# Two transformer layers on one core: statistics a block ahead, a two-phase start, and a LayerNorm apply with a negated mean

## The chip, the cores and the metric

The kernel runs on one core of one Trainium2 chip. The metric is the device time of one execution in microseconds (us). "Median" is the median of the runs of a kernel, the profiled one among them. A profile is one execution; the same program profiled twice differed by 3 us, so differences of 2 or 3 us between the ends of single traces are not read.

Names: PE is TensorE, ACT is ScalarE, DVE is VectorE, POOL is GpSimd, SP is the engine that issues DMAs.

## The reference, cut to what matters

```python
def _layernorm(x, axis=-1, eps=1e-5):
    m = jnp.mean(x, axis=axis, keepdims=True)
    v = jnp.var(x, axis=axis, keepdims=True)
    return (x - m) / jnp.sqrt(v + eps)

# A: attention, 2048 tokens, width 512, 32 heads of 16.  B: gated feed-forward, 512 -> 1792 -> 512
x = A_x
x = x + _A_ref(_layernorm(x), A_wqkv, A_wo)
x = x + _B_ref(_layernorm(x), B_w_gate, B_w_up, B_w_down)
x = x + _A_ref(_layernorm(x), A_wqkv, A_wo)          # the same weights again
x = x + _B_ref(_layernorm(x), B_w_gate, B_w_up, B_w_down)
```

The heads are tiny (16), so the exponentials of the softmax weigh as much as the matmuls (in the profile of before, ACT is busy for 1605 us and PE for 1643): 2 layers x 32 heads x 2048 x 2048 of them.

## The kernel before

The kernel is written as a list scheduler. While the program is built, a model with a cost for each instruction decides in which order each engine gets its work; that order is then fixed. PE takes its instructions strictly in that order. So a cost in the model that is too low makes PE stand in front of an instruction whose input is not there, with everything behind it waiting.

The tokens are four blocks of 512. The width is four columns of 128 (`NCK`); a column serves two "units" of a block of queries. A unit is one block of 512 queries against all keys for four heads: 64 score tiles of 128x512, numbered by key tile and head, in groups of 12 tiles (three key tiles). There are 32 units in a layer, 64 in all. A score slot takes three tiles: either ACT does the exponential of all three, or ACT does two and DVE the third (an integer approximation) when it has time. Before units 2c and 2c+1 of layer 0 can run, column c must have its projections: a key, a value and, per block of queries, a query projection. For the first block of queries that makes 4 + 4 + 1 = 9 groups of matmuls per column.

The LayerNorm and its apply (`us` is the model's cost in us; 1.05 for POOL):

```python
def stats(i, rows, key, then=None, prio=1):
    dve(prio, [(lambda e: e.bn_stats(ST[:, i, :], rows), [key], [("ST", i)], 0.72),
               (lambda e: e.bn_aggr(MV[:, i, :], ST[:, i, :]), [("ST", i)], [("MV", i)], 0.1)], then)

def ln_scale(n, then, lo=0):                  # on POOL: 1/sqrt(var + eps) into row 1
    ...
    (lambda e: e.tensor_scalar(LNS[:, 0, lo:lo + n], var, LN_EPS, None, op0=ALU.add), ...
    (lambda e: e.tensor_tensor(LNS[:, 1, lo:lo + n], LNS[:, 0, lo:lo + n], CM05[:, 0:n], op=ALU.pow), ...

def ln_apply(i, rows, key, eng, alt, then=None, us=None):
    us = us or (1.05 if eng == "pool" else 0.46)
    job(eng, 1, [(lambda e: e.tensor_scalar(xn(i, alt), rows, MV[:, i, 0:1], LNS[:, 1, i:i + 1],
                                            op0=ALU.subtract, op1=ALU.mult), ...
```

The head, which brings in the four blocks, and the projections:

```python
def head_source(b):                           # one block: statistics, scale, apply, transposes
    ...
    if b > 1:
        while ("xnt", 0, b - 2) not in have:
            yield None
    for i, tt in enumerate(tts):
        stats(i, xb(tt), ("XB", tt), got(("st", name, i)), prio=0 if b == 0 else 1)
    for lo, n in parts:
        ...                                   # wait, ln_scale, wait, ln_apply on DVE
    for i, tt in enumerate(tts):
        ...
        yield transpose_piece(...)
    have.add(("xnt", 0, b))                   # block b is in

def kv(c, b):                                 # a column's key and value projection of block b
    def gate():
        return ("xnt", layer, b) in have and (...)
```

And the choice of what PE does next. Score matmuls come first, then matmuls of weights with values if there are many, then a "piece" of something else, if it fits before the next score matmuls are due. The last number is how much a piece may delay them:

```python
if bs is None or piece_ready(p, bs) > t + 0.02 or p.cost + change("full") > limit + src.tol():
    continue
...
sources = [Source(heads(), lambda: 0.1), Source(prep_source(), lambda: 0.1), Source(post_source(), post_tol)]
```

When PE has nothing, the program gives it dummy matmuls, meant to keep its clock up (`keep_clock`, tiles `fONB,fZV`).

## Time and profile before

| | before |
|---|---|
| median of the first three runs | 1774.62 us (1772.35 to 1775.3) |
| ACT busy | 1605 us, 90% |
| PE busy, dummies included | 1643 us, 93% |
| DVE busy | 1273 us, 72% |
| first exponential, end of the last one | 21.8 us, 1701.7 us |

The list of the costliest groups on the page, cut to two. The columns are: line of the program, engine, operation, output<-input, shape, count | busy us, mean ns | idle us of the engine just before them, and what ended it.

```profile
L1139 ACT ACTIVATE fPT<-fPS 128x1024 bf16<-128x1024 f32 (+1 forms) x1440 | 1531.5, 1200 | 95.6 <-PE fPS L1134 93.5
...
L555 POOL TENSOR_SCALAR fHT<-fX,fMV,fLNS 128x512 bf16<-128x512 f32 x36 | 75.3, 2106 | 0.9
```

The exponentials are nearly all of ACT's work, and nearly all of ACT's idle time in front of them (93.5 of 95.6 us) ended with a score matmul of PE. So the question is why PE was late. The timeline of ACT at the start (start, length, group, and in brackets the idle time before it):

```profile
21.82 13.54 ACT L1139 ACTIVATE fPT<-fPS 128x1536 bf16<-128x1536 f32 x10 [9.39 <-PE fPS L1134]
40.92 8.16 ACT L1139 ACTIVATE fPT<-fPS 128x1536 bf16<-128x1536 f32 x6 [5.57 <-PE fPS L1134]
50.10 32.91 ACT L1139 ACTIVATE fPT<-fPS 128x1536 bf16<-128x1536 f32 x32 [1.01 <-PE fPS L1134]
```

Ten three-tile exponentials take 13.54 us, 1.35 us each from one to the next. There are holes of 5.57 and 1.01 us while blocks 2 and 3 come in. It is worth seeing what PE did in the longer one, from 35.4 to 40.9 us (line 585 with `fWK`: key projections, four matmuls each; line 649: value projections, sixteen each):

```profile
34.25 1.90 PE L585 MATMUL fPS<-fXNT,fWK 128*128 128x512 bf16 x8
...
35.98 1.06 PE L649 MATMUL fPS<-fWV,fXNT 128*128 128x128 bf16 x16
...
37.30 1.07 PE L649 MATMUL fPS<-fWV,fXNT 128*128 128x128 bf16 x16
...
38.62 1.04 PE L585 MATMUL fPS<-fXNT,fWK 128*128 128x512 bf16 x4
39.50 1.06 PE L649 MATMUL fPS<-fWV,fXNT 128*128 128x128 bf16 x16
```

The second place is the LayerNorms that POOL applies, nine of them. Here is the first; first POOL, then ACT, then PE's longest waits over the whole run (total us, times, longest):

```profile
263.54 8.27 POOL L555 TENSOR_SCALAR fHT<-fX,fMV,fLNS 128x512 bf16<-128x512 f32 x4
```

```profile
271.07 1.45 ACT L1139 ACTIVATE fPT<-fPS 128x1536 bf16<-128x1536 f32 x1 [2.22 <-PE fPS L1134]
273.13 1.45 ACT L1139 ACTIVATE fPT<-fPS 128x1536 bf16<-128x1536 f32 x1 [0.61 <-PE fPS L1134]
276.04 1.45 ACT L1139 ACTIVATE fPT<-fPS 128x1536 bf16<-128x1536 f32 x1 [1.45 <-PE fPS L1134]
```

```profile
PE fPS L1134 <- ACT fPT L1139: 54.0, 198, 1.1
PE fPS L562 <- POOL fHT L555: 22.1, 27, 1.6
```

Four applies take 8.27 us, about 2.07 each, where the model allows 4.2. PE stands in front of the transposes (line 562) for 22.1 us in all, the score matmuls behind them come late, and ACT stands too. The windows query of the first three of these LayerNorms (length; busy us of PE, weight load, DVE, ACT, POOL; granted clock, DMA share, GB/s) shows a lower clock there too. That it comes with the waiting is shown by E1 below, where the waiting is gone and the clock at these three LayerNorms is 1.00:

```profile
263.00:279.00 16.00, 12.63 (x104) 3.95 (x96) 4.41 (x9) 11.49 (x9) 8.70 (x5) 0.79 0.02 4
415.00:431.00 16.00, 12.81 (x93) 3.49 (x89) 5.24 (x10) 10.88 (x11) 9.13 (x5) 0.68 0.25 67
480.00:498.00 18.00, 14.35 (x113) 4.35 (x106) 3.78 (x7) 13.19 (x11) 8.27 (x4) 0.81 0.05 15
```

ACT was busy 11.49 of 16 us in the first. Added up from the trace over the 16 us after the start of each of the nine applies, ACT was idle for 31.7 us.

### The profile page before, as it was taken

To read this page: it belongs to the slowest core of one execution; us is meant where nothing else is said; L and a number is where in the kernel's file an instruction comes from. 1 tells how busy PE (TensorE), PEld (TensorE's weight loads), DVE (VectorE), ACT (ScalarE), POOL (GpSimd) and SP (SyncE) were. 2 spreads that over 40 slices of the span, in tenths; PEclk is the share of its full clock that TensorE was granted. 3 is DMA by queue.
4 is the path that set the end of the run, shared out by engine and by line. 5 is a ranking of instruction groups with operands and counts; after the bars stand their busy time and mean duration, and the time that the engine had idled before them with its cause. 6 is when DMAs were issued, how large, how long until landed. Compare 5 with 4: busy or idle time off the path is not lost.

```text
span 1774.4 us, 38110 instructions
## 1 busy us (share of the span) xinstructions
PE 1643.3 (93%) x16129; PEld 495.7 (28%) x16129; DVE 1272.6 (72%) x2117; ACT 1605.2 (90%) x1486; POOL 243.1 (14%) x200
## 2 busy tenths in 40 slices
PE   9999998998899999999999999999988999899998
PEld 4232222222222223222332222222222222222233
DVE  7799985776756976549543999668786687855853
ACT  4999998998999999999899999899988999999932
POOL 2212021102201032010610111201012000201000
PEclk9999999998999999999999999999999999999999
DMA  4100001152012420143124000014301233013503
GB/s 131 49 2 17 2 18 42 53 164 59 16 43 82 150 53 13 46 126 108 47 66 143 2 18 18 25 49 121 111 18 31 58 108 111 21 43 88 149 19 103
DMA packets 140289, 111.89 MB, mean 63 GB/s; under 512 B 13904, under 2 KB 129872, under 8 KB 140112
## 3 DMA queue, kind: packets, MB, share of 16 engines
q1 hardware_dynamic: 136416, 104.78, 20.4%
q0 software_dynamic: 2112, 4.19, 0.9%
q8 instruction: 131, 2.15, 0.5%
q10 hardware_dynamic: 1584, 0.39, 0.1%
q14 instruction: 46, 0.38, 0.1%
HBM read 97.78 MB, written 6.82 MB: 59 GB/s over the span
## 4 chain that ended last, share of the span: by engine, by line
ACT 54%; PE 28%; DVE 11%; POOL 4%; issue 1%; DMA 1%; SPq 0%; POOLq 0%; DVEq 0%
ACT fPT L1139 50%; PE fPS L585 8%; PE fPS L1134 7%; PE fPS L1244 5%; DVE fPI L1173 5%; DVE fPP L1195 3%; POOL fHT L555 3%; PE fPS L943 3%; PE fPS L1264 3%; ACT fHT L1105 2%; DVE fQ L629 1%; PE fPS L649 1%; PE fPS L562 1%; POOL fLNS L545 1%; ACT L1105 1%
## 5 line engine op out<-in xcount | busy, mean ns | idle before, releaser
L1139 ACT ACTIVATE fPT<-fPS 128x1024 bf16<-128x1024 f32 (+1 forms) x1440 | 1531.5, 1200 | 95.6 <-PE fPS L1134 93.5
L1134 PE MATMUL fPS<-fQ,fKT 32*128 32x512 bf16 x4096 | 557.3, 388 | 69.3 <-ACT fPT L1139 54.0
L1173 DVE TENSOR_SCALAR fPI<-fPS 128x512 int16<-128x512 f32 x772 | 506.9, 683 | 89.4 <-PE fPS L1134 87.6
L1244 PE MATMUL fPS<-fPT,fVP 128*17 128x512 bf16 x3324 | 437.8, 388 | 3.8 <-DVE fPP L1195 2.0
L1195 DVE TENSOR_SCALAR fPP<-fPI 128x2048 int16<-128x2048 int16 x579 | 391.7, 711 | 6.6 <-PE fPS L1244 5.5
L1134 PEld LDWEIGHTS fPS<-fQ,fKT 32*128 32x128 bf16 x4096 | 139.6, 91 | 612.8 <-ACT fPT L1139 508.3
L1244 PE MATMUL fPS<-fPP,fVD 128*17 128x512 f16 x2316 | 297.7, 383 | 8.3 <-DVE fPP L1195 7.5
L1264 PE MATMUL fPS<-fONB,fZV 128*17 128x512 bf16 x3124 | 243.6, 389 | 2.4 <-POOL fQMASK L361 1.5
L585 PE MATMUL fPS<-fXNT,fWR 128*128 128x512 bf16 x896 | 232.2, 388 | 11.9 <-DVE fHT L929 9.0
L1244 PE MATMUL fPS<-fPI,fVP 128*17 128x512 f16 x772 | 214.3, 384 | 0.9 <-DVE fPP L1195 0.8
L929 DVE TENSOR_TENSOR fHT<-fPS,fHT 128x512 bf16<-128x512 f32 x112 | 76.9, 689 | 112.5 <-PE fPS L585 78.9
L778 POOL TENSOR_TENSOR fAT<-fOS,fRB 128x512 bf16<-128x512 f32 x32 | 40.9, 1278 | 814.5 <-DMA fRB<-rscr 814.5
L1244 PEld LDWEIGHTS fPS<-fPT,fVP 128*17 128x17 f16 x3324 | 98.9, 87 | 166.7 <-issue 125.3
L906 DVE CAST fHT<-fPS 128x512 bf16<-128x512 f32 x98 | 67.6, 690 | 96.2 <-PE fPS L585 96.2
L943 PE MATMUL fPS<-fWR,fHT 128*128 128x512 bf16 x448 | 123.6, 383 | 0.4
L585 PEld LDWEIGHTS fPS<-fXNT,fWR 128*128 128x128 bf16 x896 | 72.7, 98 | 130.0 <-DVE fHT L929 27.4
L1244 PEld LDWEIGHTS fPS<-fPP,fVD 128*17 128x17 f16 x2316 | 70.2, 88 | 94.1 <-issue 44.4
L1264 PEld LDWEIGHTS fPS<-fONB,fZV 128*17 128x17 f16 x3124 | 72.2, 91 | 75.8 <-issue 33.0
L555 POOL TENSOR_SCALAR fHT<-fX,fMV,fLNS 128x512 bf16<-128x512 f32 x36 | 75.3, 2106 | 0.9
L662 POOL TENSOR_SCALAR fVD<-fVP 128x544 f16<-128x544 f16 (+1 forms) x48 | 53.4, 1115 | 137.8 <-DVE fVP L670 135.1
L576 DVE COPY fXNT<-fPS 128x512 bf16<-128x512 bf16 x62 | 25.2, 422 | 61.9 <-PE fPS L562 61.7
L543 POOL TENSOR_SCALAR fLNS<-fMV 128x4 f32<-128x4 f32 (+1 forms) x17 | 7.6, 444 | 451.3 <-DVE fMV L537 451.3
(59 smaller groups left out, 732.6 us busy)
## 6 DMA issues: line engine op xcount, KB each, us to landing
fWR<-in_B_w_down_dram SPq DMA_DIRECT2D x189, 256.0 KB, 3.0
fWR<-in_B_w_gate_dram SPq DMA_DIRECT2D x56, 256.0 KB, 3.3
fWR<-in_B_w_up_dram SPq DMA_DIRECT2D x56, 256.0 KB, 2.8
fRB<-rscr SPq DMA_DIRECT2D x256, 32.0 KB, 1.9
fX<-in_A_x_dram POOLq DMA_DIRECT2D x4, 1024.0 KB, 5.7
xscr<-fX SPq DMA_DIRECT2D x16, 256.0 KB, 2.5
fX<-xscr SPq DMA_DIRECT2D x4, 1024.0 KB, 5.5
fAT<-fATS SPq DMA_DIRECT2D x128, 16.0 KB, 1.8
```

What stands on the lines that cost most here:

```text
L555: job(eng, 1, [(lambda e: e.tensor_scalar(xn(i, alt), rows, MV[:, i, 0:1], LNS[:, 1, i:i + 1], op0=ALU.subtract, op1=ALU.mult), [key, ("MV ...
L585: ins = e.matmul(bank(bs[0])[:, 0:cols], lhsT=l, rhs=r_, start=(i == 0), stop=(i == n - 1))
L662: job("pool", 2, [(lambda e, dst=dst, src=src, ph=ph: e.tensor_scalar(dst, src, 2.0 ** (-ph / NPH), None, op0=ALU.mult), [("VP", c, k) for ...
L906: evac_job(1, b, [(lambda e: e.tensor_copy(HT[:, ft, :], bank(b)), [BK[b]], [("HT", ft)], 0.6)], got(("gate", layer, qb, ft)))
L929: (lambda e: e.tensor_tensor(HT[:, ft, :], bank(b), HT[:, ft, :], op=ALU.mult), [BK[b], ("HT", ft)], [("HT", ft)], 0.62)], got(("up", laye ...
L943: ins = e.matmul(bank(b)[:, 0:D], lhsT=HT[:, ft, i * 128:(i + 1) * 128], rhs=WR[:, s, jj * D:(jj + 1) * D], start=(ft == 0), stop=(ft == N ...
L1134: ins = e.matmul(bank(b0 + k), lhsT=KT[32 * j:32 * j + 32, c, kt * 128:(kt + 1) * 128], rhs=Q[32 * j:32 * j + 32, qs, :], start=True, stop ...
L1139: o = sch.op("act", lambda e: e.activation(PT[:, p, 0:512 * na].rearrange("p (a b) -> p a b", a=na), PS[:, b0:b0 + na, :], ACTF.Exp, scale ...
L1173: dve(0, [(lambda e: e.tensor_scalar(PI[:, gi, 512 * r:512 * (r + 1)], bank(b0 + n - 1), DBIAS, 0.0, op0=ALU.add, op1=ALU.max), [bks[-1]], ...
L1195: shifts.append((s, [(lambda e: e.tensor_scalar(PP[:, s, :], PI[:, gi, :], int(OCT) * ph // NPH, None, op0=ALU.add), [("PI", gi, r) for r ...
L1244: ins = e.matmul(PS[32 * j:32 * j + VW, ACC, :], lhsT=l, rhs=r_, start=a, stop=z, tile_position=(0, 32 * j), skip_group_check=True)
L1264: ins = e.matmul(PS[32 * j:32 * j + VW, ACC, :], lhsT=ZV[:, :], rhs=ones, start=False, stop=False, tile_position=(0, 32 * j), skip_group_c ...
```

## The change

Its intent: bring the blocks in sooner and start the exponentials sooner. Statistics of a block are taken while the block before is worked on. The first two units do their first 12 tiles each before either goes on, so 24 tiles wait only for block 0. The score banks are kept for the scores once the first query projection is there. The second column's projections wait until all four blocks are in. DVE helps with exponentials only once all four blocks are in, where before it could from the second unit on. And the LayerNorm apply becomes add,multiply with a row that holds minus the mean, which costs one small POOL instruction per LayerNorm.

```diff
-    ST = sb("fST", [128, 4, 6], F32)           (MV and LNS likewise: 4 -> 8)
+    ST = sb("fST", [128, 8, 6], F32)
...
         pool_ -= held3
+        if slot_no[0] < 2 and (0, "q", 0) in have:
+            pool_.difference_update(slot_banks())
...
     def ln_scale(n, then, lo=0):
+        mean = AP(MV, 2 * lo, [[16, 128], [2, n]])
...
+            (lambda e: e.tensor_scalar(LNS[:, 2, lo:lo + n], mean, -1.0, None, op0=ALU.mult),
+             keys + [("LNS", lo + i) for i in range(n)], [("LNS", lo + i) for i in range(n)], 0.3)], then)
...
-        job(eng, 1, [(lambda e: e.tensor_scalar(xn(i, alt), rows, MV[:, i, 0:1], LNS[:, 1, i:i + 1],
-                                                op0=ALU.subtract, op1=ALU.mult),
-                      [key, ("MV", i), ("LNS", i)], [xnkey(i, alt)], us)], then, ported=True)
+        job(eng, 1, [(lambda e: e.tensor_scalar(xn(i, alt), rows, LNS[:, 2, st + i:st + i + 1], LNS[:, 1, st + i:st + i + 1],
+                                                op0=ALU.add, op1=ALU.mult),
+                      [key, ("LNS", st + i)], [xnkey(i, alt)], us)], then, ported=True)
...
+    def started_all():
+        return ("xnt", 0, NQB - 1) in have
...
-        def kv(c, b):
+        def kv(c, b, after_all=False):
             def gate():
-                return ("xnt", layer, b) in have and (
+                return ("xnt", layer, b) in have and (not after_all or started_all()) and (
...
-                return ("xnt", layer, up // NCK) in have and filled_units[0] >= layer * NU + 2 * up + 2 - NQS
+                return ("xnt", layer, up // NCK) in have and (layer or not up or started_all()) and filled_units[0] >= ...
...
-                    kv(up, b)
+                    kv(up, b, layer == 0)
...
-        if layer and NQB > 1:
-            for u in us[:NPART]:
-                unit(u, "A", 0, NMA, False)
...
+        if NQB > 1:
+            np_, m = (NPART, NMA) if layer else (2, 1)
+            for u in us[:np_]:
+                unit(u, "A", 0, m, False)
+            for u in us[:np_]:
+                unit(u, "B", m, NM, 4 * NKT > 12 * NM)
+            us = us[np_:]
...
-            d = size == 3 and (layer or u) and vector_group() and behind() < LAG
+            d = size == 3 and started_all() and vector_group() and behind() < LAG
...
+    def head_stats(b):
+        for i in range(4):
+            tt = 4 * b + i
+            stats(i + 4 * (b % 2), xb(tt), ("XB", tt), got(("st", ("head", b), i)), prio=2 if b else 0)
...                                            (head_source: its own statistics and the wait for block b - 2 go; the model's cost of its apply, 0.2, becomes 0.35)
+        if b + 1 < NQB:
+            head_stats(b + 1)
```

More of the change, by code (lines that the diff above doesn't have):

```diff
@@ L244, in _emit_fast @@
     ATS = sb("fATS", [128, 2, 512], BF)
-    ST = sb("fST", [128, 4, 6], F32)
-    MV = sb("fMV", [128, 4, 2], F32)
-    LNS = sb("fLNS", [128, 3, 4], F32)
+    ST = sb("fST", [128, 8, 6], F32)
+    MV = sb("fMV", [128, 8, 2], F32)
+    LNS = sb("fLNS", [128, 3, 8], F32)
     OKL = sb("fOKL", [128, 128], F32)
@@ L540, in ln_scale @@
         keys = [("MV", lo + i) for i in range(n)]
-        var = AP(MV, 2 * lo + 1, [[8, 128], [2, n]])
+        mean = AP(MV, 2 * lo, [[16, 128], [2, n]])
+        var = AP(MV, 2 * lo + 1, [[16, 128], [2, n]])
         job("pool", 1, [
@@ L545, in ln_scale, with ln_apply @@
             (lambda e: e.tensor_tensor(LNS[:, 1, lo:lo + n], LNS[:, 0, lo:lo + n], CM05[:, 0:n], op=ALU.pow),
-             [("LNS", lo + i) for i in range(n)] + [("CM05",)], [("LNS", lo + i) for i in range(n)], 1.1)], then)
+             [("LNS", lo + i) for i in range(n)] + [("CM05",)], [("LNS", lo + i) for i in range(n)], 1.1),
+            (lambda e: e.tensor_scalar(LNS[:, 2, lo:lo + n], mean, -1.0, None, op0=ALU.mult),
+             keys + [("LNS", lo + i) for i in range(n)], [("LNS", lo + i) for i in range(n)], 0.3)], then)
     def ln_check(n):
-        var = AP(MV, 1, [[8, 128], [2, n]])
+        var = AP(MV, 1, [[16, 128], [2, n]])
         dve(2, [(lambda e: e.scalar_tensor_tensor(OKV[:, 0:n], var, L_HI, OKV[:, 0:n], op0=ALU.is_le, op1=ALU.mult),
                  [("MV", i) for i in range(n)] + [("OKV",)], [("OKV",)], 0.1)])
-    def ln_apply(i, rows, key, eng, alt, then=None, us=None):
+    def ln_apply(i, rows, key, eng, alt, then=None, us=None, st=0):
         us = us or (1.05 if eng == "pool" else 0.46)
-        job(eng, 1, [(lambda e: e.tensor_scalar(xn(i, alt), rows, MV[:, i, 0:1], LNS[:, 1, i:i + 1],
-                                                op0=ALU.subtract, op1=ALU.mult),
-                      [key, ("MV", i), ("LNS", i)], [xnkey(i, alt)], us)], then, ported=True)
+        job(eng, 1, [(lambda e: e.tensor_scalar(xn(i, alt), rows, LNS[:, 2, st + i:st + i + 1], LNS[:, 1, st + i:st + i + 1],
+                                                op0=ALU.add, op1=ALU.mult),
+                      [key, ("LNS", st + i)], [xnkey(i, alt)], us)], then, ported=True)
     def transpose_piece(i, tt, alt=False, eng="dve", then=None):
@@ L697, in gate @@
             def gate():
-                return ("xnt", layer, up // NCK) in have and filled_units[0] >= layer * NU + 2 * up + 2 - NQS
+                return ("xnt", layer, up // NCK) in have and (layer or not up or started_all()) and filled_units[0] >= layer * NU + 2 * up + 2 - NQS
             add(gate, lambda: qproj(layer, up))
@@ L1017, in unit @@
                 groups.append((layer, u, part, 12 * m1, 4 * NKT - 12 * m1, None, True))
-        if layer and NQB > 1:
-            for u in us[:NPART]:
-                unit(u, "A", 0, NMA, False)
-            for u in us[:NPART]:
-                unit(u, "B", NMA, NM, 4 * NKT > 12 * NM)
-            us = us[NPART:]
+        if NQB > 1:
[5 more added lines that the diff above has]
+            us = us[np_:]
         for u in us:
@@ L1276, in head_source @@
         alt = b % 2 if NFT >= 8 else 0
+        st = 4 * (b % 2)
         name = ("head", b)
-        if b > 1:
-            while ("xnt", 0, b - 2) not in have:
-                yield None
         parts = [(0, 2), (2, 2)] if b == 0 else [(0, 4)]
-        for i, tt in enumerate(tts):
-            stats(i, xb(tt), ("XB", tt), got(("st", name, i)), prio=0 if b == 0 else 1)
         for lo, n in parts:
@@ L1286, in head_source @@
                 yield None
-            ln_scale(n, got(("lns", name, lo)), lo)
+            ln_scale(n, got(("lns", name, lo)), lo + st)
             while ("lns", name, lo) not in have:
@@ L1290, in head_source @@
             for i in range(lo, lo + n):
-                ln_apply(i, xb(tts[i]), ("XB", tts[i]), "dve", alt, got(("xn", name, i)), us=0.2)
+                ln_apply(i, xb(tts[i]), ("XB", tts[i]), "dve", alt, got(("xn", name, i)), us=0.35, st=st)
+        if b + 1 < NQB:
+            head_stats(b + 1)
         for i, tt in enumerate(tts):
@@ L1303, in heads @@
     def heads():
+        head_stats(0)
         for b in range(NQB):
```

## The prediction

> **What bounds it now.** The page's busy table gives ScalarE (ACT) 1605 of 1774 us (90%); the chain that ended last is 50% exponentials (1497 ns for three tiles, 1068 for two). The list of groups has 95.6 us of idle before them, 93.5 waiting for score matmuls. The timeline of ACT places it:
> - Head: first exponential at 21.8 us, holes of 5.6 us at 35.4 and 1.0 at 49.1. Unit 0 eats a block's keys in groups of 12 tiles (5.4 us); a new block took about 11.5 us (statistics start at 12.4, 23.2, 34.4).
> - Nine LayerNorms applied on GpSimd (POOL). The waits show PE held 22.1 us by POOL's apply (27 times). It takes 2081 ns (least 2072, so not contention); the schedule in the program allows 1.05 us. PE takes its transposes in order, so the score matmuls behind them are late. In the 16 us from six of these (263, 415, 480, 1127, 1337, 1548) ACT idles 4 to 5 us, over all nine about 31. The windows of the first three show a granted clock of 0.68 to 0.81; the Trainium skill, "TensorE: Matmul & The Clock Gate", Part 1, has half rate after idle windows, which agrees.
> - Tail: last exponential ends at 1701.7, 73 us before the end.
>
> **The change, part by part.**
> 1. Statistics a block ahead: about 3.2 us of DVE leave each block's chain. Key evacuation for block 0 no longer queues behind them (matmul 12.6, evacuation 15.6).
> 2. Score banks held back once Q is there, second-column projections put off until all blocks are in: the first score matmul waited from Q ready (17.5) to 21.4. First exponential at 16 to 17 us: -5.
> 3. Two units in two phases: 24 tiles (10.8 us) of block-0 work before block 1 is needed. Blocks 1, 2, 3 should be in by about 24, 31, 38; needed at about 27, 33, 43. The 6.6 us of holes nearly close: -6. Cost: two evacuations of 0.68 us on DVE.
> 4. Negated mean: one more POOL instruction (0.25 us) per LayerNorm, and add,multiply for subtract,multiply. On DVE no difference expected (0.34 us). On POOL no line of the trace shows the new form; the bet is that it is about twice as fast. For: other POOL costs in the schedule fit (pow 1.1 against 1.04, tensor-tensor 1.35 against 1.27), and the program's general path already pays for a negated row. The Trainium skill, "GPSIMD Engine Reference", 3.1, gives 768 ns for 512 elements at best; the trace's 2081 does not agree. Against: scaling by a constant (1.63) is slower than scheduled too (1.08). I give it 0.75. If so, stalls and clock dips at the nine LayerNorms mostly go: -26. If not, nothing there.
>
> **Sum.** ACT bounds nearly everything between head and tail, so these add: -11 head, -26 LayerNorm, about 1738 us; without the POOL gain about 1764. The rest of the schedule is reshuffled: a few us either way.
>
> **Signs.** First exponential at 16 to 17; no ACT hole over 2 us before 60; POOL apply 1.0 to 1.2 us; PE's wait for it under 5 us; granted clock near 1.00 in those windows; ACT idle before exponentials down from 95 to about 55; tail still about 73 us.
>
> **What would make it wrong.** POOL apply still 2.1 us; block 1 late; reshuffling that opens new holes at the layer change (6.4 us at 861 now) or in the tail.
>
> 2% is 1739: nearly even. Faster 0.52, same 0.47, slower 0.01; range 1724 to 1767.

## The result, and the profile after

| | before | after |
|---|---|---|
| median of four runs | 1774.96 us | 1750.42 us (1747.28 to 1756.33) |
| ratio | | 0.9864 (95%: 0.9832 to 0.9896) |
| mean granted clock in the profile | 0.982 | 0.996 |
| first exponential | 21.8 us | 17.1 us |
| end of the last exponential | 1701.7 us | 1678.7 us |

A ratio compares the runs of the same rounds and is not quite the ratio of the medians. The kernel is 24.5 us faster by the medians, 1.4%, within the range (its middle is 1745.5) and 12 us above the 1738 of the sum. It is a change within 2%: "same", to which I had given 0.47, and "faster" 0.52.

The groups of after that answer to those of before:

```profile
L1149 ACT ACTIVATE fPT<-fPS 128x1024 bf16<-128x1024 f32 (+1 forms) x1440 | 1529.1, 1216 | 74.2 <-PE fPS L1144 72.0
```

The POOL apply has fallen out of the page's list. Asked for its line, the trace says (duration in ns: least, median, most):

```profile
L560 POOL TENSOR_SCALAR fHT<-fX,fLNS x36: 767/772/775, 277.6 to 1534.0; 128x512 bf16<-128x512 f32 x36
L560 DVE TENSOR_SCALAR fHT<-fX,fLNS x28: 397/412/548, 8.1 to 1705.2; 128x512 bf16<-128x512 bf16 x16, 128x512 bf16<-128x512 f32 x12
```

2081 ns have become 772, on the same shape and types. On DVE the same instruction did not change (median 410 before, 412 after). The windows at the same LayerNorms, and PE's waits, of which the one for POOL's apply is gone:

```profile
277.00:293.00 16.00, 15.01 (x140) 4.88 (x132) 4.87 (x9) 16.00 (x13) 3.45 (x6) 1.00 0.12 34
421.00:437.00 16.00, 14.31 (x132) 3.97 (x132) 9.76 (x18) 14.83 (x14) 3.88 (x5) 0.85 0.24 67
482.00:500.00 18.00, 16.66 (x147) 5.22 (x139) 5.81 (x10) 18.00 (x15) 3.28 (x5) 1.00 0.11 30
```

```profile
PE fPS L1144 <- ACT fPT L1149: 55.7, 205, 1.1
PE fPS L1254 <- DVE fPP L1205: 11.0, 20, 1.7
```

ACT is busy 16 of 16 us and 18 of 18 in two of the three. Over the nine applies its idle time, added up as before, is 2.1 us instead of 31.7. That alone is more than the whole gain. So something was lost elsewhere, and the timeline of ACT at the start shows where:

```profile
17.12 12.37 ACT L1149 ACTIVATE fPT<-fPS 128x1536 bf16<-128x1536 f32 x9 [3.90 <-PE fPS L1144]
32.15 6.82 ACT L1149 ACTIVATE fPT<-fPS 128x1536 bf16<-128x1536 f32 x5 [2.65 <-PE fPS L1144]
41.12 30.16 ACT L1149 ACTIVATE fPT<-fPS 128x1536 bf16<-128x1536 f32 x30 [2.15 <-PE fPS L1144]
81.79 42.26 ACT L1149 ACTIVATE fPT<-fPS 128x1024 bf16<-128x1024 f32 x44 [10.50 <-PE fPS L1144]
128.10 2.85 ACT L1149 ACTIVATE fPT<-fPS 128x1024 bf16<-128x1024 f32 x3 [4.05 <-PE fPS L1144]
...
177.62 1.02 ACT L1149 ACTIVATE fPT<-fPS 128x1024 bf16<-128x1024 f32 x1 [5.25 <-PE fPS L1144]
...
230.90 3.77 ACT L1149 ACTIVATE fPT<-fPS 128x1024 bf16<-128x1024 f32 x4 [3.15 <-PE fPS L1144]
```

The first exponential is 4.7 us sooner and the head's holes are smaller (4.8 us instead of 6.6), but at 71, 124, 172 and 228 us there are new holes of 23.0 us together (before had one of 1.9 us in this stretch, at 169). The first three are the starts of units 2, 4 and 6, where a new column begins. What PE did in the longest of them:

```profile
73.81 1.07 PE L654 MATMUL fPS<-fWV,fXNT 128*128 128x128 bf16 x16
74.71 1.03 PE L590 MATMUL fPS<-fXNT,fWK 128*128 128x512 bf16 x4
75.57 1.06 PE L654 MATMUL fPS<-fWV,fXNT 128*128 128x128 bf16 x16
76.47 1.03 PE L590 MATMUL fPS<-fXNT,fWK 128*128 128x512 bf16 x4
77.33 1.06 PE L654 MATMUL fPS<-fWV,fXNT 128*128 128x128 bf16 x16
78.22 1.03 PE L590 MATMUL fPS<-fXNT,fWQ 128*128 128x512 bf16 x4
79.09 1.03 PE L590 MATMUL fPS<-fXNT,fWK 128*128 128x512 bf16 x4
79.95 1.06 PE L654 MATMUL fPS<-fWV,fXNT 128*128 128x128 bf16 x16
81.35 0.39 PE L1144 MATMUL fPS<-fQ,fKT 32*128 32x512 bf16 x3 [0.34 <-DVE fKT L644]
```

It did the second column's projections, one after the other, each about 0.9 us from one to the next, until DVE had brought out the query and the last keys and unit 2 could start. In before they had been done earlier. Counted from the matmul records: of the 39 projections that run before unit 10 in every version, 23 had started in before when the last score matmul of unit 1 was issued, in after only 10; ten more followed in the hole. This count is what the table below and the texts call the projections done at unit 2, or when unit 2 starts.

A useful measure from here on is the start of the k-th score matmul, because there are 4096 of them in every version and the order of units is nearly the same. The first of unit 10 starts at 260.3 us in before and at 269.0 in after: the head, with a start 4.7 us sooner, is 8.7 us behind. All the rest of the run is 34 us shorter (37 in the second profile of after, E11).

### The profile page after: what moved, and what is told of

The parts are those of the page before. It is cut to its first block, busy times and chain, and to the rows that moved or that the text cites. A ratio compares the mean times of both kernels' runs of the same rounds, so it can differ in the third digit from the quotient of the medians. Undisturbed runs are those within 1.5% of the kernel's fastest.

```text
span 1749.1 us, 38353 instructions
## 1 busy us (share of the span) xinstructions
PE 1635.7 (94%) x16245; PEld 494.1 (28%) x16245; DVE 1270.9 (73%) x2105; ACT 1602.8 (92%) x1486; POOL 199.4 (11%) x217
## 4 chain that ended last, share of the span: by engine, by line
ACT 67%; PE 23%; DVE 8%; issue 1%; POOL 0%; DMA 0%; SPq 0%; DVEq 0%; POOLq 0%
ACT fPT L1149 64%; PE fPS L590 6%; PE fPS L1144 5%; PE fPS L1254 5%; PE fPS L1274 3%; DVE fPI L1183 3%; DVE fPP L1205 3%; ACT fHT L1115 2%; PE fPS L951 2%; PE fPS L654 1%; DVE fQ L634 1%; ACT L1115 1%; ACT L1149 0%; PE fPS L567 0%; DVE fOS L827 0%
## 5 line engine op out<-in xcount | busy, mean ns | idle before, releaser
L1149 ACT ACTIVATE fPT<-fPS 128x1024 bf16<-128x1024 f32 (+1 forms) x1440 | 1529.1, 1216 | 74.2 <-PE fPS L1144 72.0
L1183 DVE TENSOR_SCALAR fPI<-fPS 128x512 int16<-128x512 f32 x764 | 501.5, 684 | 66.5 <-PE fPS L1144 64.9
L1254 PE MATMUL fPS<-fPP,fVD 128*17 128x512 f16 x2292 | 301.9, 381 | 6.0 <-DVE fPP L1205 5.4
L1274 PE MATMUL fPS<-fONB,fZV 128*17 128x512 bf16 x3264 | 251.1, 385 | 2.4 <-POOL fQMASK L361 1.5
L590 PE MATMUL fPS<-fXNT,fWR 128*128 128x512 bf16 x896 | 226.7, 381 | 10.2 <-DVE fHT L937 5.9
L590 PEld LDWEIGHTS fPS<-fXNT,fWR 128*128 128x128 bf16 x896 | 71.9, 97 | 123.2 <-DVE fHT L937 21.6
L827 DVE COPY fOS<-fPS 128x512 f32<-128x512 f32 x64 | 43.8, 684 | 24.4 <-PE fPS L1254 24.2
```

What stands on the lines that cost most here:

```text
L590: ins = e.matmul(bank(bs[0])[:, 0:cols], lhsT=l, rhs=r_, start=(i == 0), stop=(i == n - 1))
L1149: o = sch.op("act", lambda e: e.activation(PT[:, p, 0:512 * na].rearrange("p (a b) -> p a b", a=na), PS[:, b0:b0 + na, :], ACTF.Exp, scale ...
L1183: dve(0, [(lambda e: e.tensor_scalar(PI[:, gi, 512 * r:512 * (r + 1)], bank(b0 + n - 1), DBIAS, 0.0, op0=ALU.add, op1=ALU.max), [bks[-1]], ...
L1254: ins = e.matmul(PS[32 * j:32 * j + VW, ACC, :], lhsT=l, rhs=r_, start=a, stop=z, tile_position=(0, 32 * j), skip_group_check=True)
L1274: ins = e.matmul(PS[32 * j:32 * j + VW, ACC, :], lhsT=ZV[:, :], rhs=ones, start=False, stop=False, tile_position=(0, 32 * j), skip_group_c ...
```

## The experiments

Theory A: the time of the POOL apply depends on the operation. Theories C, E and H: the parts at the head gain nothing in the end, because the holes of ACT in the head of before were the time in which PE did the later columns' projections. Rivals are given with each run. "Before" was run in the same rounds each time: E1 to E4 share their rounds (before 1775.61), so do E5 to E8 (1776.03) and E9 to E11 (1775.26). Between these groups a difference of 1 or 2 us is not read. E2, E5 and E6 were counted as wrong with relative errors of 0.020005, 0.0200010 and 0.0200018, just above what was accepted; their arithmetic for one element is that of before, but which tiles DVE's approximation gets depends on the order. That this is the reason was not tested.

| run | median us | ratio to before | POOL apply ns | first exponential us | projections done at unit 2 | holes over 1 us up to 260 us | unit 10 against before | end against before |
|---|---|---|---|---|---|---|---|---|
| before | 1775 | 1 | 2081 | 21.8 | 23 | 8.5 | 0 | 0 |
| after | 1750.4 | 0.9864 | 772 | 17.1 | 10 | 27.7 | +8.7 | -25.3 |
| E1 | 1741.1 | 0.9810 | 767 | 21.4 | 23 | 8.5 | -0.5 | -36.1 |
| E2 | 1746.1 | 0.9830 | 767 | 38.8 | 30 | 4.3 | +10.4 | -28.5 |
| E3 | 1784.9 | 1.0057 | 2081 | 16.1 | 10 | 28.0 | +9.4 | +6.8 |
| E4 | 1741.2 | 0.9804 | 767 | 16.9 | 15 | 24.4 | +7.5 | -33.2 |
| E5 | 1736.4 | 0.9776 | 772 | 22.3 | 23 | 8.5 | +0.1 | -39.4 |
| E6 | 1743.2 | 0.9820 | 772 | 16.7 | 12 | 23.5 | +6.5 | -33.9 |
| E7 | 1746.3 | 0.9835 | 767 | 21.6 | 19 | 20.5 | +8.9 | -30.5 |
| E8 | 1740.2 | 0.9799 | 768 | 16.7 | 16 | 9.6 | -2.1 | -39.6 |
| E9 | 1733.9 | 0.9767 | 770 | 17.4 | 21 | 5.8 | -4.1 | -41.8 |
| E10 | 1739.0 | 0.9795 | 769 | 17.0 | 14 | 11.5 | +0.5 | -39.0 |
| E11 (after again) | 1749.1 | 0.9854 | 767 | 17.3 | 10 | 27.8 | +8.8 | -28.5 |

The holes are sums of ACT's idle stretches over 1 us between the first exponential and 260 us. The projections are counted when the last score matmul of unit 1 is issued. The last two columns are in us, from the profiled run of each against the profile of before: the start of unit 10's first score matmul, and the end.

### E1: the operation alone

```diff
-                                                op0=ALU.subtract, op1=ALU.mult),
+                                                op0=ALU.add, op1=ALU.mult),
```

Still with the mean from its old place.

> The kernel before with one letter of meaning changed: the LayerNorm apply adds the mean from its old place instead of subtracting it (the result is wrong on purpose, slightly, since the means are small). No instruction is added, and the order of all instructions is that of before. Theory A (GpSimd's time depends on the operation, add against subtract): the apply takes about 0.76 us as after, PE's wait for GpSimd goes from 22 us to under 2, and the time falls by 28 to 35 us, to 1740 to 1747. Rival B (it is reading both scalars from the same tile, or the extra row, that makes it fast): the apply stays at 2.08 us and the time at 1775.

The relative error was 0.65, so my "slightly" was wrong: the means are not small in all the LayerNorms. For the time that does not matter. The line of the apply in this run, and the page's line of the exponentials:

```profile
L555 POOL TENSOR_SCALAR fHT<-fX,fMV,fLNS x36: 759/767/1295, 263.1 to 1519.4; 128x512 bf16<-128x512 f32 x36
L1139 ACT ACTIVATE fPT<-fPS 128x1024 bf16<-128x1024 f32 (+1 forms) x1440 | 1527.7, 1209 | 65.5 <-PE fPS L1134 63.6
```

Same tiles, same operands, same order on all engines: 767 ns instead of 2081. PE's wait for POOL's apply went from 22.1 us to 0.2, ACT's idle time at the nine applies from 31.7 to 1.4; the clock in the windows at the first three is 1.00 (0.79, 0.68 and 0.81 in before). The time fell by 34.6 us (medians of the same rounds, 1775.61 to 1741.06). Theory A is shown, rival B is out. The score matmuls show the gain in steps: nothing up to unit 10, 4.9 us from there to unit 11, 5.4 from 15 to 16, 5.4 from 18 to 19, and so on, each at a POOL LayerNorm.

### E2: the negated row alone

```diff
+            (lambda e: e.tensor_scalar(LNS[:, 2, lo:lo + n], mean, -1.0, None, op0=ALU.mult), ...
-  rows, MV[:, i, 0:1], LNS[:, 1, i:i + 1], op0=ALU.subtract, op1=ALU.mult
+  rows, LNS[:, 2, i:i + 1], LNS[:, 1, i:i + 1], op0=ALU.add, op1=ALU.mult
```

> The kernel before with the negated row and add,multiply alone, nothing of the head. Theory A with C (the parts at the head bring nothing in the end, as what they gain by unit 2 is lost there): 1745 to 1753, about the time of after. Rival D (the parts at the head do bring 6 us or more): 1755 to 1762. The extra GpSimd instruction also moves the plan of the whole kernel; if 1753 and E1 at 1742 differ by 8 or more, the extra instruction costs that in the head.

Measured 1746.1 us, ratio 0.983: the case of A with C. So the whole gain of the change, and 3 to 5 us more, comes from this part. The surprise is in the timeline of ACT:

```profile
38.79 95.64 ACT L1142 ACTIVATE fPT<-fPS 128x1536 bf16<-128x1536 f32 x91 [25.28 <-PE fPS L1137]
```

The extra instruction moves the plan: PE runs 19 projections between 13.8 and 33.5 us, before the first score matmul at 38.4, and the first exponential comes 17.4 us later than in E1. (That the projections took the score banks is my reading of the program; the trace does not show the banks.) Yet the run ends only 5 us later than E1. PE did 30 projections before unit 2, and ACT then runs without a hole for 95 us. When the first exponential starts says little about the end.

### E3: the parts at the head alone

```diff
 (after, with)
-  rows, LNS[:, 2, st + i:st + i + 1], LNS[:, 1, ...], op0=ALU.add, op1=ALU.mult
+  rows, MV[:, st + i, 0:1], LNS[:, 1, ...], op0=ALU.subtract, op1=ALU.mult      and no third row
```

> The kernel after with the apply put back to subtract,multiply from the mean, without the negated row; all the parts at the head stay. Theory C: GpSimd's apply is back at 2.08 us, PE waits about 22 us for it, the first exponential is at about 17 us, the hole of about 10 us at the start of unit 2 is there, and the time is 1773 to 1783: no gain. Rival D: 1762 to 1768.

Measured 1784.9 us, ratio 1.0057: 9 us slower than before by the medians, a little above what theory C allowed (1773 to 1783), and far from rival D. The first exponential is at 16.1 us, the earliest of all, and the hole at unit 2 is there:

```profile
16.14 18.91 ACT L1146 ACTIVATE fPT<-fPS 128x1536 bf16<-128x1536 f32 x14 [3.46 <-PE fPS L1141]
38.35 30.22 ACT L1146 ACTIVATE fPT<-fPS 128x1536 bf16<-128x1536 f32 x30 [3.30 <-PE fPS L1141]
79.30 42.26 ACT L1146 ACTIVATE fPT<-fPS 128x1024 bf16<-128x1024 f32 x44 [10.72 <-PE fPS L1141]
```

E1 and E3 multiply to 0.981 x 1.0057 = 0.9866, which is what after measured (0.9864 and 0.9854). The change is the sum of a gain of about 34 us and a loss of about 10.

### E4: the putting off of keys and values undone

```diff
-                    kv(up, b, layer == 0)
+                    kv(up, b)
```

> The kernel after, but the second column's key and value projections may again start when their own block is in, as before the change (its query projection stays put off). Theory E (putting them off makes the 10.5 us hole at 71 us: nine matmul groups of about 1 us must run before unit 2 can start): the hole shrinks under 3 us, the start of unit 2 comes 6 to 10 us sooner, and the time is 1740 to 1747. Rival F (PE has no room there whatever the order, or the loss moves to a later unit): the holes only move and the time stays at 1748 to 1753.

The time is where theory E put it, 1741.2 us, but not for its reason. The hole at unit 2 shrank from 10.5 to 6.4 us only, the hole at unit 4 grew to 6.5, unit 2 starts 3.4 us sooner than in after where 6 to 10 were expected, and unit 10 just 1.3 us sooner. The profile of E4 ends 4.7 us before that of E11, and most of it is made between the starts of units 10 and 16: this stretch is 154.2 us long instead of 158.6, because DVE does the exponentials of 72 tiles in it instead of 56, and ACT is busy for 151.6 us instead of 158.2. So it is another split of the exponentials between the engines, well after the hole. The mechanism in E's form (this one gate makes the hole) is not confirmed by this run; 15 projections at unit 2 instead of 10 are still too few.

### E5: the fast operation only where POOL applies

```diff
+        off, op0 = (LNS[:, 2, i:i + 1], ALU.add) if eng == "pool" else (MV[:, i, 0:1], ALU.subtract)
...                                         (the third row is made only for these nine LayerNorms)
```

> The kernel before, with the negated row and add,multiply only in the nine LayerNorms that GpSimd applies; the head is that of before, with no added instruction. If the operation is all that part 4 does, it keeps the head of before (first exponential 21 to 22 us, about 23 of the 39 projections of the first four columns done when unit 2 starts) and runs in 1735 to 1743 us, about the time of E1 and 8 to 14 below after, with a right result. If the reshuffling by the extra instruction costs as in E2: 1744 to 1750.

Measured 1736.4 us, inside the range; the head is that of before (23 projections at unit 2, unit 10 at +0.1 us). It is 14 us below after without any of the parts at the head. Only its relative error, 0.0200010, keeps it from being the version to take. It is also 4.7 us below E1 although the heads are alike. The two ran in different rounds. At the start of unit 59 their profiles are 0.7 us apart, at the end 3.3; what makes this difference was not taken apart. It is the size of what can come from elsewhere than the head.

### E6: the putting off alone

```diff
 (E5, with kv(up, b, layer == 0), the gates on started_all() for kv and q, as in the change)
```

> E5 plus only the putting off of the second column's projections until all four blocks are in. Theory E: with fewer than 16 projections done when unit 2 starts, ScalarE gets holes of together over 8 us at the starts of units 2, 4 and 6, and the time is 4 to 10 us above E5. Rival G (putting off frees VectorE and brings the blocks in sooner, so the head gains what unit 2 loses): within 3 us of E5.

Measured 1743.2 us, 6.8 above E5. With 12 projections at unit 2 there are holes of 7.9, 6.7 and 2.1 us at units 2, 4 and 6:

```profile
79.68 42.20 ACT L1146 ACTIVATE fPT<-fPS 128x1024 bf16<-128x1024 f32 x44 [7.86 <-PE fPS L1141]
128.56 1.02 ACT L1146 ACTIVATE fPT<-fPS 128x1024 bf16<-128x1024 f32 x1 [6.68 <-PE fPS L1141]
...
177.04 4.79 ACT L1146 ACTIVATE fPT<-fPS 128x1024 bf16<-128x1024 f32 x5 [2.08 <-PE fPS L1141]
```

This part alone brings the first exponential from 22.3 to 16.7 us, and loses more than that by unit 4. Rival G is out.

### E7: the two phases alone

```diff
 (E5, with the first two units of layer 0 in phases "A" and "B", as in the change)
```

> E5 plus only the two phases of the first two units. Theory H (the holes of ScalarE in the head of before were no loss: PE did the later columns' projections in them; filling them with exponentials only moves them to the starts of units 2, 4 and 6): the head's hole at 35 us goes, later ones come, and the time is 2 to 9 us above E5. Rival G (filling the holes is a gain of about 5): 3 to 6 us below E5.

Measured 1746.3 us, 9.9 above E5 and just outside theory H's 2 to 9, on the side away from rival G. The hole at 35 us went, as expected, and came back as holes of 3.0 and 7.1 us at 39 and 43 us and of 6.6 at unit 4:

```profile
50.51 37.00 ACT L1144 ACTIVATE fPT<-fPS 128x1536 bf16<-128x1536 f32 x36 [7.14 <-PE fPS L1139]
131.63 1.02 ACT L1144 ACTIVATE fPT<-fPS 128x1024 bf16<-128x1024 f32 x1 [6.60 <-PE fPS L1139]
```

I had predicted this part to gain 6 us. Two limits of this run: it keeps before's rule for when DVE helps, so DVE takes its first four exponentials at 26 to 29 us (at 48 us in after, at 57 in E5), and this is not quite the two phases as the change has them. And the hole of 7.1 us is not theory H's: after the one at 41.8 us PE starts no projection until 50.6, but transposes, dummies and matmuls of weights with values that wait for POOL and DVE. The loss against E5 is only 1.3 us at the start of unit 2 and 6.6 at that of unit 4.

### E8: room for the projections

```diff
-    sources = [Source(heads(), lambda: 0.1), Source(prep_source(), lambda: 0.1), ...
+    sources = [Source(heads(), lambda: 0.1), Source(prep_source(), lambda: 0.4), ...
```

> The kernel after with one number changed: a projection may delay the next score matmuls by 0.4 us instead of 0.1, so that it fits between two-tile exponentials. Theory E with H (PE has room in sum, as its dummy matmuls show, but no slot is long enough for a projection of 0.9 to 1.0 us while VectorE helps): over 14 projections are done when unit 2 starts instead of 10, the holes at units 2, 4, 6 and 9 (23 us together in after) fall by more than half, and the time is 1735 to 1744. Rival F: the same delay in smaller pieces, 1747 to 1755.

Measured 1740.2 us, with a right result. 16 projections are done at unit 2, the 23.0 us of holes after 60 us have become 5.2:

```profile
74.97 1.02 ACT L1149 ACTIVATE fPT<-fPS 128x1024 bf16<-128x1024 f32 x1 [1.81 <-PE fPS L1144]
154.39 42.20 ACT L1149 ACTIVATE fPT<-fPS 128x1024 bf16<-128x1024 f32 x44 [3.38 <-PE fPS L1144]
```

Unit 10 starts at 258.1 us instead of 269.0, with everything else of the change kept. So PE had the time. The dummy matmuls say the same: up to unit 10 there were 584 in before, 688 in after, 584 in E8. What was missing was a slot long enough. From the traces: a two-tile exponential comes every 0.96 us (42.26 us for 44, in after), the score matmuls take 0.3 of that and a projection 0.9, so it cannot go in without a delay of about 0.24 us; with three tiles on ACT (1.35 us) it fits. While DVE helps, ACT does two. A projection that is not put in costs ACT its full 0.9 us later, when the unit cannot start. This arithmetic is an estimate from those numbers; the 0.1 and 0.4 us of the program are in the model's costs, so they can't be set against it directly. That more room for projections removes most of the holes is measured.

### E9: a version from these findings

```diff
-                    kv(up, b, layer == 0)
+                    kv(up, b)
-            d = size == 3 and started_all() and vector_group() and behind() < LAG
+            d = size == 3 and (layer or u) and vector_group() and behind() < LAG
-    sources = [..., Source(prep_source(), lambda: 0.1), ...
+    sources = [..., Source(prep_source(), lambda: 0.15), ...
```

> The version put together from what the runs showed: after, with the second column's key and value projections free to start with their block, VectorE helping from the second unit on whatever blocks are in (as in before), and a projection allowed to delay the score matmuls by 0.15 us instead of 0.1. Expected: at least 18 projections done when unit 2 starts, holes over 1 us before unit 10 under 8 us together after the first exponential, and 1732 to 1739 us with a right result: below after by 10 to 18 and no slower than E5. If the first units cannot be had cheaper than in before: 1736 to 1742, the same as E8.

Measured 1733.9 us, ratio 0.9767 (0.975 to 0.9784), with a right result: 2.3% faster than before and 15 us faster than after in the same rounds. 21 projections are done at unit 2. After 42 us ACT has no hole over 1 us until 837 us, near the layer change:

```profile
33.89 6.82 ACT L1149 ACTIVATE fPT<-fPS 128x1536 bf16<-128x1536 f32 x5 [4.29 <-PE fPS L1144]
42.26 84.45 ACT L1149 ACTIVATE fPT<-fPS 128x1536 bf16<-128x1536 f32 x81 [1.54 <-PE fPS L1144]
```

Here the earlier start is kept: unit 10 is 4.1 us ahead of before. Whether that is the worth of the parts at the head is not shown: before's head with more room for projections (E5 with 0.15 us) was not run, and the ratios of E9 and E5, 0.9767 and 0.9776, overlap in their intervals.

### E10: another size of the same room

```diff
-    sources = [..., Source(prep_source(), lambda: 0.1), ...
+    sources = [..., Source(prep_source(), lambda: 0.15), ...
```

> E8 with 0.15 us in place of 0.4 us, nothing else changed from after. If E8's gain is the room for projections and not one lucky order of instructions, this quite different order gains too: more than 14 projections done when unit 2 starts, 1734 to 1743 us. If E8 was luck: 1746 to 1753.

Measured 1739.0 us, ratio 0.9795. 14 projections at unit 2, where I had expected more than 14; holes of 11.5 us. Two sizes of room, and nearly the same gain: that speaks against E8 as one lucky order.

### E11: after again

> The kernel after, unchanged, on the same chip and in the same rounds as E9 and E10, to compare with: 1747 to 1753 us.

Measured 1749.1 us (1747.67 to 1750.26), ratio 0.9854. The holes are those of the first profile of after, each to 0.1 us.

## Why the prediction was right or wrong

The range held and the time was within it, but two terms of the sum were off, in opposite directions: the LayerNorm brought 8 to 9 us more than its 26, and the head lost about 9 where 11 were to be gained, 20 us worse. That the errors partly cancelled, so that the sum missed by 12 us only, was luck.

- *"-26 LayerNorm"*: right in the mechanism, too small in size. The bet that add,multiply runs faster on POOL than subtract,multiply was right, and E1 shows that it is the operation and nothing else. It is 2.7 times as fast (2081 over 772 ns), not twice, and where it was alone (E1) it brought 34.6 us. I had counted 31 us of ACT's idle time and then taken off a part that did not need taking off: in E1 30.3 of 31.7 us went. The rest of E1's gain is in the page's line of the exponentials: their idle time fell by 30.1 us and their busy time by 3.8 (1531.5 to 1527.7), together nearly all of the 34.3 us by which the last one ends sooner.
- *"-11 head"*: wrong, in sign too. This is the step that failed. It had two parts, "-5" for the first exponential and "-6" for the holes. The first exponential did come at 17.1 us as predicted. But I took a hole of ACT in the head for lost time. PE was not idle in it: it did the later columns' projections, and with ACT at full speed and DVE helping too few of them fit between the score matmuls. E3 measured the head at +9 to +10 us, E6 its putting off at +6.8, E7 its two phases (with an earlier help of DVE) at +9.9 over E5; these are not to be added. With room for the projections, unit 10 starts 2.1 us (E8) and 4.1 us (E9) before that of before instead of 8.7 after it. At the end of the run neither is shown to be faster than E5, which has none of these parts.
- *"ACT bounds nearly everything between head and tail, so these add"*: this held for the LayerNorm gain, whose steps in the score matmuls stay to the end, and for the sum of E1 and E3. It did not hold for the start of the exponentials: E2 started 17 us late and lost 5.
- *"Blocks 1, 2, 3 should be in by about 24, 31, 38"*: late. Block 1's keys were projected at 29.9 us, and block 3's about 44. Between the evacuations of block 1's transposes DVE did the next block's statistics and the extra evacuation of the first phase, and PE ran at half clock there, as the window shows (which of them cost how much was not tested):

```profile
25.90:29.30 3.40, 3.40 (x34) 1.00 (x35) 1.93 (x5) 3.33 (x3) 1.51 (x3) 0.50 0.01 2
```

- *Signs*: first exponential at 16 to 17 (17.1, right); no hole over 2 us before 60 (wrong: 2.65 and 2.15); POOL apply 1.0 to 1.2 us (0.77); PE's wait for it under 5 us (0 after, right); clock near 1.00 in those windows (1.00, 0.85, 1.00: nearly); ACT's idle time before exponentials from 95 to about 55 us (74.2, wrong: the new holes); tail about 73 us (70.4).
- *"reshuffling that opens new holes at the layer change or in the tail"*: new holes came, but at the starts of units 2, 4 and 6, and not by an unlucky order alone: E11 reproduces them, E3 has them too, E6 makes holes at the same three places, and E8 takes most of them away.

What stays open: why the program gives DVE 56 tiles between units 10 and 16 in after and 72 in E4; and what before's head would gain from room for the projections. After unit 10, the fast-apply versions are 36 to 41 us shorter than before (after 34 in one profile and 37 in the other), and no run took this spread of some 5 us apart beyond E4's share.

On the Trainium skill: "GPSIMD Engine Reference", 3.1, gives 768 ns predicted and 769 measured as the best case of 512 elements on POOL, and I read the trace's 2081 as a reason to hope. The runs' 767 to 772 ns for add,multiply agree with it. "TensorE: Matmul & The Clock Gate", Part 1, has the clock at half after an idle window of about 3.4 us. The half clock and the length of the window just shown, 3.4 us at 0.50, agree; the word idle does not: in the 3.4 us before it PE was busy for 2.1 us. The prediction's "which agrees" has the same limit.

## What to carry to other kernels

Compare the cost that a planner assumes for each instruction with the trace; one that is twice too low, in front of an engine that takes its work in order, shows as waiting of quite other engines, and a mere change of operation can repair it. A hole of the engine that bounds the kernel is lost time only if no other engine used it for work that is needed later: before filling it, ask what the others did in it and where that work will go. And judge a faster start by a mark well past it, like the start of the tenth unit, not by when the first result appears.

## What the Trainium skill lacked or had wrong

- "GPSIMD Engine Reference", 3.1: the page does not say that the time of a two-step instruction with per-partition scalars depends on the operation. On 128x512, f32 to bf16, add,multiply took 767 to 772 ns and subtract,multiply 2081 (medians of 36 each; E1 changes only the operation). Its figure for the best case agrees with add,multiply.
- "TensorE: Matmul & The Clock Gate", Part 1: the table of states has half rate after an idle window of about 3.4 us and gives no share of PE work up to which a window counts as idle. In after, half clock at 25.9 us followed 3.4 us in which PE was busy for 2.1 us (61%), with no gap over 1 us.
